# Fourier convolution with real and imaginary parts side by side, complex sums on VectorE and the inverse in row tiles

## The chip, the core and the metric

The kernel runs on one core of one Trainium2 chip. The metric is the time of one execution on the device in microseconds (us); the median of three runs stands for a kernel. The core has five engines that run their own queues in order and meet by semaphores: TensorE (PE, with its weight loads shown as PEld), VectorE (DVE), ScalarE (ACT), GpSimd (POOL) and SyncE (SP, here an issuer of DMAs). On-chip data lie in SBUF, and products of PE in the eight banks of PSUM, in both cases on 128 partitions.

## The reference

A block with two halves on 2048 rows of 576 channels: an S4 convolution and a gated MLP, each ahead of a residual and under scales from `c`. Cut to what matters here:

```python
mod = (_silu(c) @ w_mod).reshape(c.shape[0], 6, 1, -1)
h = _layernorm(x) * (1 + ca) + sa
P = exp(logdA[:, :, None] * l); K = einsum("dn,dnl,dn->dl", Cc, P, dB).real
Kf = rfft(pad(K, L)); Uf = rfft(pad(h.T, L))
y = irfft(Uf * Kf)[:L].T + h * Dskip          # L = 2048, transforms of 2L
x = x + ga * y
h = _layernorm(x) * (1 + cb) + sb
z = _gelu(h @ w_in); z1, z2 = z[..., :Fh], _layernorm(z[..., Fh:])   # Fh = 2304
x = x + gb * ((z1 * (w_sp @ z2 + b_sp)) @ w_out)
```

The change is in `y`: the transform of `h`, its complex product with `Kf`, and the inverse.

## The kernel before

Two parts follow one another. `ssm` (line 235) does the first residual, class `Mlp` the second, in `phase_a` (line 1370: layer norm, the second half of `w_in`, gelu, its layer norm) and `phase_b` (line 2149: the large products). The convolution is done in fp32 on PE as transforms in two steps, in five groups of channels (four of 128, one of 64) and in units, each a generator that stops at its `yield`s:

- e, t, p, k ("kg"), 1 ("k1") make the kernel's spectrum from the poles: exponentials and sines on ScalarE, `pg` products on VectorE, small products on PE (lines 561 to 690). They share time with the units below.
- `u_load`, `u_unit` (lines 706 and 711): a block of 512 columns (frequencies times channels) of the half-transformed `h` comes from DRAM as `u1`; one product with `fwd`, 128x128, gives the real parts in partitions 0 to 63 and the imaginary in 64 to 127 of a `pk` bank. ScalarE copies it into `uu[:, 0]`, and two DMAs from GpSimd's queue write the two halves swapped into `uu[:, 1]`.
- `z_unit` (line 722): the kernel's spectrum for the same 512 columns, products of `cst` with `k1`, into a `pk` bank; VectorE multiplies it with `uu` and with the swapped `uu` into `zz`, 128x1024.
- `v_unit` (line 733): two products over 512 columns with all 128 partitions of input, `inva` with `zz[:, 0]` and `invb` with `zz[:, 1]`, add up in one bank: the signs and sums of the complex product lie in the matrices (`st3a`, `st3b` in `consts`, line 131). ScalarE copies the bank to `v`, and a DMA of GpSimd's queue stores it in DRAM (`v_d`).
- `y_vload`, `y_xload`, `y_unit` (lines 745 to 790): SP's queue loads `v_d` again by rows, PE makes pairs of 128x64 products (in the records 128*64), VectorE adds them to `x`, and the sum goes to DRAM as `x1`; in the last groups of channels it also stays in SBUF (`x1f`, `x1l`, `xz`), so that phase A can start.

There are 36 units each of u, z and v (eight for a group of 128 channels, four for the last) and 20 of y.

The order is written out: string `ORDER` names one step after another, `Steps` (line 849) runs the unit named to its next `yield`, and `Pin` (line 212) keeps each engine's instructions in that order. All of them have the helper's line in the profile, L222, so one reads by tiles. Step D0 ends the making of the spectrum and starts `Mlp`. Steps L0 to L17 (list `late`) put first pieces of phase A among the last u, z, v and y: loads of `w_in` (`start_load`), its column sums and power-of-two scales (`start_sum`, `win_scale`), and its split in two fp16 parts (`start_hi` on ScalarE, `start_lo` on VectorE). The rest of these pieces stands at the start of `phase_a`, after `turn(0)`, the transposes of the first row tile. Which buffer of a ring each unit takes is written out too, in `PLAN`, by `Rings` (line 194): `uu` has four buffers of 128x2x512, `zz` two, `pk` four PSUM banks of 128x512.

Of the kernel before, what the change touches and what calls it, by code (L numbers as in the profile page):

```python
# [9 lines left out]
F32 = mybir.dt.float32  # L10
# [22 lines left out]
    "et": "0123401230243102431042341203420143201",  # L33
    "ft": "012012012120120210121021012102021021",
    "k1": "0101010",
    "kab": "010101001101010101001000111010110101",
    "pg": "010101101010101010110010101011010101",
    "pk": "01230123230123010123230130213020132013201320132013201023102312031203120312031203120312031202031203120312031023"
        "10231023102310231032132103210310210230210321031201321320130132103210230120120132120123102310312012301021302130"
        "12023013021013021301203123123023102023021321021302031203132103102312031203102310231023012312012031021302310231"  # L40
        "0231203121023120312013213201230130101010101010101010101010101010101010101",
    "ps": "01011011010101010101001010101111110101010101101010101011001101010110101010010101010101010101010101010101010101"
        "0101",
    "st1o": "010101010101010101",
    "u1": "0123401342304234130140320420124412032142102432402102401031024130",
    "uu": "01231032030313020231013020122030120123120",
    "v": "0101101010101101011010101010101010",
    "xb": "01100100101",
    "zz": "01011110110111010101010101101011011010",
# [3 lines left out]
B0 O0 O0 O0 O0 B2 O0 O0 O0 O0 B7 O0 O0 O0 O0 x0 O0 O0 O0 O0 O0 B1 O0 O0 O0 O0 O0 O0 S0 O0 O0 S0 i2 P0 S0 O0 O0 P0 O0 O0 B3 M2 S0 O0 P0 B5 Q0 i1 S0 M2 P0 S0 P0 e1 e0 P0 P0  # L53
e1 B6 P0 e0 B4 i0 e1 e0 t0 e1 g0 t1 M2 e0 P0 t1 t1 w3 M1 M1 M1 P0 P0 t2 M2 P0 M0 M1 M3 R1 R0 t1 t0 P0 t0 M0 M0 p1 t2 P0 p1 t0 p1 t2 j1 t2 e5 w4 M0 e2 M3 M3 p0 M0 p0 M0 e2
k1 p0 k1 e2 e2 k0 P0 M3 e3 11 M0 e5 P0 M0 11 11 O0 k0 M4 S1 e3 e5 p2 p2 g1 S1 M4 P0 S1 p2 e3 e6 M0 M4 e5 k2 O0 e4 e6 M3 P0 P0 e3 k2 M4 S1 A0 A0 R3 e4 R2 A0 t3 P0 A0 A0 A0
S1 A1 t3 S1 t5 A1 t3 O0 A1 A1 t5 A0 A1 A1 r2 t3 A1 t4 R5 A2 t5 A2 A2 R4 A2 e7 p3 A2 A2 A3 P0 t5 p3 P0 A3 M4 t4 r3 P0 A3 A3 10 p3 A3 t4 O0 A3 e8 12 R7 A2 j2 10 P0 e6 O0 t4
10 12 e4 p5 e7 k3 e4 e6 t8 12 k3 R6 e7 e7 A4 A4 A3 p5 e8 p5 t8 A4 p4 A4 A4 e8 e8 A4 S2 t7 A5 t8 S2 P0 A5 P0 A5 A5 S2 S2 S2 A5 P0 P0 A5 A4 t7 t7 P0 A6 t8 A6 A6 p4 t6 p4 A6
O0 A6 A6 A5 a5 t6 t6 A7 A7 A7 k4 t7 R10 a4 A7 R11 A7 A7 P0 k4 P0 13 w5 t6 13 14 Q1 13 P0 e10 p7 A6 14 k5 p7 A7 14 p7 M5 k7 e9 x3 e10 k5 M5 R8 P0 e11 k7 A8 e11 R9 p6 A8 A8
S3 A8 t10 A8 A8 S3 t10 S3 e9 S3 A9 A9 A9 A9 A9 e11 S3 p6 e10 r6 e10 p6 e9 t11 e9 A9 e11 Q2 A10 A10 R13 R12 p8 t10 A8 A10 A10 P0 A10 A10 17 k6 A9 p8 17 t11 p8 17 t10 M5 k6
t9 M5 t11 A11 A11 p10 t11 A11 P0 A10 e12 A11 15 A11 r7 t9 O0 p10 R15 t9 15 p10 A11 15 k8 k8 O0 A12 A12 e14 e12 p11 A11 p11 A12 A12 A12 A12 t14 A13 t14 A13 e14 P0 A13 M5  # L60
# [24 lines left out]
def consts():  # L85
# [46 lines left out]
    for h, sg in ((0, 1.0), (1, -1.0)):  # L132
        rows = slice(64 * h, 64 * h + 64)
        st3a[rows, 0::2] = sg * tr
        st3a[rows, 1::2] = -sg * ti
        st3b[rows, 0::2] = ti
        st3b[rows, 1::2] = tr
# [97 lines left out]
def ssm(tc, I, x1_d, consts_s, dram, mod_d, mlp):  # L235
# [6 lines left out]
    with ExitStack() as ctx:  # L242
# [314 lines left out]
        et = {}  # L557
# [1678 lines left out]
```

## Time and profile before

| | us |
|---|---|
| median of 3 runs (lowest to highest) | 1744.23 (1741.78 to 1744.63) |
| profiled execution, its own time | 1742.69 |
| its span | 1740.5 |
| PE busy | 1649.0 (95%) |
| VectorE busy | 1231.1 (71%) |
| ScalarE busy | 834.6 (48%) |
| GpSimd busy | 249.4 (14%) |

The span is what the profiler sees of the profiled execution, 2.2 us less than its time. "Busy" counts instructions that compute; a share over the whole span hides that the kernel has stages with different limits, so the stages must be read apart. In rows of the timeline a name such as `pk_b<-zz_b,small` is the output and the inputs, `128*64` the tile of PE, `x4` the number of records: an fp32 product has two.

### The profile page before, as it was taken

How to read it: one execution, taken by the hardware profiler on the slowest of the kernel's cores; microseconds unless marked ns; L12 is line 12 of the kernel's file. 1: busy time of each engine (PE TensorE's matmuls, PEld its weight loads, DVE VectorE, ACT ScalarE, POOL GpSimd, SP SyncE). 2: the span in 40 equal slices, each digit the busy share in tenths (PEclk: the TensorE clock that was granted, in tenths of full speed). 3: DMA queues.
4: the chain of work that ended last, by engine and by line, in shares of the span. 5: the costliest groups of instructions: out<-in, count | busy, mean ns of one | idle time of the engine just before them, and what ended most of it. 6: DMA issues, size and time to landing. Idle time of an engine off the chain costs nothing.

```text
span 1740.5 us, 38338 instructions
## 1 busy us (share of the span) xinstructions
PE 1649.0 (95%) x16158; PEld 1235.7 (71%) x16158; DVE 1231.1 (71%) x2179; ACT 834.6 (48%) x1202; POOL 249.4 (14%) x412
## 2 busy tenths in 40 slices
PE   3778999997999999999999999999999999999999
PEld 1344556664555446877878888888888888888887
DVE  6976888857999997888897867786444387334442
ACT  6979898762777565455443434343221233112210
POOL 3251323332222110000000000000111100111100
PEclk9878999998999999999999999999999999999999
DMA  9475946698798788676757786764667563556531
GB/s 240 141 214 179 276 118 202 198 292 242 226 308 265 227 249 294 243 250 241 248 161 237 273 298 241 266 213 144 241 225 234 197 217 105 194 198 213 194 108 42
DMA packets 182940, 376.43 MB, mean 216 GB/s; under 512 B 39104, under 2 KB 102976, under 8 KB 182000
## 3 DMA queue, kind: packets, MB, share of 16 engines
q1 hardware_dynamic: 138304, 168.56, 31.7%
q0 software_dynamic: 37984, 178.55, 31.1%
q10 hardware_dynamic: 6480, 26.86, 3.8%
q8 instruction: 127, 2.08, 0.5%
q14 instruction: 45, 0.37, 0.1%
HBM read 263.18 MB, written 101.31 MB: 209 GB/s over the span
## 4 chain that ended last, share of the span: by engine, by line
PE 66%; DVE 15%; DMA 6%; issue 3%; ACT 2%; POOL 0%; SPq 0%; ACTq 0%; DVEq 0%; POOLq 0%
PE ps L222 56%; PE pk_a L222 3%; PE pk_d L222 2%; PE pk_b L222 2%; DVE bsz L222 2%; DMA zset<-set_d 2%; PE pk_c L222 2%; DVE n L222 1%; DVE zset L222 1%; DVE rq L222 1%; DVE wsp L222 1%; DVE wso L222 1%; DVE gt L222 1%; DMA v_d<-v_a 1%; DVE nt L222 1%
## 5 line engine op out<-in xcount | busy, mean ns | idle before, releaser
L222 PEld LDWEIGHTS <-zset 128*128 128x128 f16 x7182 | 702.7, 98 | 92.4 <-DVE zset L222 7.2
L222 PE MATMUL ps<-wsp,zset 128*128 128x256 f16 x6048 | 669.0, 273 | 6.3 <-DVE zset L222 5.5
L222 PE MATMUL pz<-wz,nt 128*128 128x512 f16 (+1 forms) x1120 | 223.7, 359 | 8.9 <-ACT nt L222 3.5
L222 ACT ACTIVATE z<-gt 128x1024 f16<-128x1024 f32 x56 | 59.0, 1054 | 283.9 <-DVE gt L222 283.9
L222 PEld LDWEIGHTS <-nt 128*128 128x128 f16 x1120 | 109.4, 99 | 117.0 <-issue 5.0
L1944 POOL DMA_DIRECT2D zset<-set_d x96 | 50.8, 530 | 869.3 <-PE ps L222 608.1
L222 DVE SCALAR_TENSOR_TENSOR gt<-ps,sc,bsp 128x512 f32<-128x512 f32 x36 | 27.0, 749 | 205.4 <-PE ps L222 203.7
L222 PE MATMUL ps<-wout,z 128*128 128x288 f16 x1344 | 170.0, 286 | 0.0
L222 PEld LDWEIGHTS <-z 128*128 128x128 f16 x1344 | 131.5, 98 | 33.0
L222 PE MATMUL ps<-n2o,zset 128*128 128x256 f16 x1134 | 128.2, 273 | 0.0
L222 DVE TENSOR_TENSOR raw<-raw 128x512 f32<-128x512 f32 (+2 forms) x228 | 119.2, 528 | 12.0 <-DMA raw<-z_d 7.6
L222 DVE SCALAR_TENSOR_TENSOR gt<-ps,sc,gt 128x512 f32<-128x512 f32 (+1 forms) x180 | 122.2, 696 | 7.6
L222 ACT ACTIVATE zset<-raw 128x1792 f16<-128x1792 f32 x48 | 81.2, 1691 | 59.6 <-PE ps L222 25.0
L222 DVE TENSOR_TENSOR zset<-raw,zset 128x1792 f16<-128x1792 f32 x48 | 97.0, 2020 | 14.9 <-ACT zset L222 12.6
L222 DVE TENSOR_TENSOR z<-ps,z 128x512 f32<-128x512 f32 (+1 forms) x126 | 72.0, 599 | 36.8 <-ACT z L222 26.7
L222 ACT ACTIVATE wsp<-raw,sc 128x1792 f16<-128x1792 f32 x25 | 44.6, 1785 | 42.7 <-DVE raw L222 35.0
L222 ACT ACTIVATE z<-z,sc 128x1024 f32<-128x1024 f32 x21 | 24.1, 1148 | 75.6 <-DVE z L222 71.9
L222 ACT ACTIVATE z<-z,nm,r 128x1152 f32<-128x1152 f32 x24 | 31.5, 1342 | 53.6 <-DVE nm L222 30.3
L222 ACT ACTIVATE z<-pz,sc 128x512 f32<-128x512 f32 (+1 forms) x96 | 51.6, 583 | 10.2 <-DMA z_d<-z 7.2
L222 PE MATMUL ps<-n2q,wf 128*128 128x512 f16 x252 | 55.7, 379 | 0.0
L222 PE MATMUL ps<-wout,z1b 128*128 128x288 f16 x384 | 52.4, 286 | 0.0
L222 DVE SCALAR_TENSOR_TENSOR wsp<-raw,sc,wsp 128x1792 f16<-128x1792 f32 x25 | 51.9, 2078 | 0.0
(700 smaller groups left out, 2591.6 us busy)
## 6 DMA issues: line engine op xcount, KB each, us to landing
zset<-set_d POOLq DMA_DIRECT2D x96, 896.0 KB, 5.0
raw<-z_d SPq DMA_DIRECT2D x48, 512.0 KB, 5.5
set_d<-zset ACTq DMA_DIRECT2D x24, 896.0 KB, 6.1
z_d<-z POOLq DMA_DIRECT2D x32, 576.0 KB, 9.3
zset<-wa_d POOLq DMA_DIRECT2D x18, 896.0 KB, 4.9
raw<-in_w_spT SPq DMA_DIRECT2D x25, 512.0 KB, 4.5
set_d<-zset SPq DMA_DIRECT2D x12, 896.0 KB, 5.8
wst<-in_w_in SPq DMA_DIRECT2D x8, 1024.0 KB, 11.8
```

The costliest lines, as they stand in the source:

```text
L222: return self.tc.keep_in_program_order(f(*a, **k))
L1944: self.nc.gpsimd.dma_start(o, self.set_d[f, j - 1] if j else self.wa_d[f])
```

## The change

Real and imaginary parts now lie side by side in the free dimension, and the two halves of the 512 columns on the two halves of the partitions. For u, PE makes four products of 64 output rows over 256 columns; the copy to `uu` (now 128x512, eight buffers) is all that follows, and no DMA swaps. For z there are likewise products of 64 rows, twice as many. VectorE multiplies real and imaginary part of the spectrum with both parts of `uu` into `zz` (128x1024 as before), and after a further `yield` subtracts and adds quarters of it in place, 128x256 each. For v only the summed half of `zz` is read: four products with 64 partitions of input over 256 columns, two for each half of the partitions, in two `pk` banks, and two copies of 256 columns by ScalarE. The signs go out of `st3a`. The strings `ORDER` and `PLAN` are new, and seven pieces of phase A's start (`start_lo(2)`, `start_load(4)`, `start_sum(3)`, `win_scale(8)`, `start_hi(3)`, `ln2_two(1)` and its roots) become steps L18 to L24 in the convolution's last part. Of the two strings the diff shows a line or two.

```diff
@@ -30,55 +30,55 @@
 ROUNDED = set(range(14)) | set(range(15, 36, 2))
...
-    "uu": "01231032030313020231013020122030120123120",
+    "uu": "0123456710325076134052135170526047326034725136",
-    "zz": "01011110110111010101010101101011011010",
+    "zz": "01010010101100101001010101010101001101",
...
 ORDER = """
-u30 k32 133 k32 135 135 X10 132 135 u34 U24 v27 132 U32 132 y5 v26 D0 L4 L5 u24 U33 v27 u30 z34 v26 u24 L2 L9 v27 z30 z34 X16 u35 z30 z24 u24 u25 L3 v30 L0 v34 u35 z24
+v28 132 132 135 v28 135 v31 W8 135 z26 y8 W10 z27 D0 X17 L2 L0 z26 v27 y8 z26 L3 v27 z34 v26 z34 L4 v28 z24 z34 z24 v26 L5 z30 y10 z24 v34 L9 v34 z30 y10 z35 X18 z30 v26
...
@@ -129,10 +129,10 @@
     th = -2 * np.pi * np.outer(b4, k2) / 64
     tr, ti = np.cos(th).T, np.sin(th).T
     st3a, st3b = np.zeros((128, 128)), np.zeros((128, 128))
-    for h, sg in ((0, 1.0), (1, -1.0)):
+    for h in range(2):
         rows = slice(64 * h, 64 * h + 64)
-        st3a[rows, 0::2] = sg * tr
-        st3a[rows, 1::2] = -sg * ti
+        st3a[rows, 0::2] = tr
+        st3a[rows, 1::2] = -ti
         st3b[rows, 0::2] = ti
         st3b[rows, 1::2] = tr
     eye = np.eye(8)
@@ -688,13 +688,8 @@
         def part(n, bufs=2):
             return ring(sb, [128, 512], F32, n, bufs)
 
-        spare = []
-
         def half():
-            if not spare:
-                uu = ring(sb, [128, 2, 512], F32, "uu", 4)
-                spare.extend((uu[:, 1], uu[:, 0]))
-            return spare.pop()
+            return ring(sb, [128, 512], F32, "uu", 8)
 
         def by(t, c):
             return t.rearrange("p (k d) -> p k d", d=CHW[c])
@@ -711,34 +706,48 @@
         def u_unit(k):
             u1 = st.pop(k)
             pm = ps1()
-            T.matmul(pm, fwd, u1, start=True, stop=True)
+            for r in range(2):
+                for q in range(2):
+                    T.matmul(pm[64 * q:64 * q + 64, 256 * r:256 * r + 256], fwd[:, 64 * r:64 * r + 64], u1[:, 256 * q:256 * q + 256],
+                             start=True, stop=True, skip_group_check=True)
             yield
-            uu = st[k] = ring(sb, [128, 2, 512], F32, "uu", 4)
-            A.activation(uu[:, 0], pm, AF.Copy)
-            yield
-            G.dma_start(uu[:64, 1], uu[64:, 0])
-            G.dma_start(uu[64:, 1], uu[:64, 0])
+            uu = st[k] = ring(sb, [128, 512], F32, "uu", 8)
+            A.activation(uu, pm, AF.Copy)
 
         def z_unit(n):
             c, i = place(n)
             w = CHW[c]
             pm = ps1()
-            for j, k in enumerate(range(32)[kr(c, i)]):
-                T.matmul(pm[:, w * j:w * j + w], cst[k // 8][:, k % 8], k1t[c][:, k, :w], start=True, stop=True)
+            ks = range(32)[kr(c, i)]
+            m = len(ks) // 2
+            for j in range(m):
+                for r in range(2):
+                    for q in range(2):
+                        k = ks[m * q + j]
+                        T.matmul(pm[64 * q:64 * q + 64, 256 * r + w * j:256 * r + w * j + w], cst[k // 8][:, k % 8, 64 * r:64 * r + 64], k1t[c][:, k, :w],
+                                 start=True, stop=True, skip_group_check=True)
             yield
             uu = st.pop(n)
             zz = st[n] = ring(sb, [128, 2, 512], F32, "zz", 2)
-            V.tensor_tensor(zz, pm[:, None, :].to_broadcast([128, 2, 512]), uu, op=ALU.mult)
+            kk, u = (t.rearrange("p (r f) -> p r f", r=2) for t in (pm, uu))
+            p = zz.rearrange("p i (j f) -> p i j f", j=2)
+            V.tensor_tensor(p, kk[:, :, None, :].to_broadcast([128, 2, 2, 256]), u[:, None, :, :].to_broadcast([128, 2, 2, 256]), op=ALU.mult)
+            yield
+            V.tensor_tensor(p[:, 0, 0], p[:, 0, 0], p[:, 1, 1], op=ALU.subtract)
+            V.tensor_tensor(p[:, 0, 1], p[:, 0, 1], p[:, 1, 0], op=ALU.add)
 
         def v_unit(n):
             c, i = place(n)
             zz = st.pop(n)
-            pm = ps1()
-            T.matmul(pm, inva, zz[:, 0], start=True, stop=False)
-            T.matmul(pm, invb, zz[:, 1], start=False, stop=True)
+            pm = [ps1(), ps1()]
+            for r, m in enumerate((inva, invb)):
+                for q in range(2):
+                    rows = slice(64 * q, 64 * q + 64)
+                    T.matmul(pm[q][:, :256], m[rows], zz[rows, 0, 256 * r:256 * r + 256], start=not r, stop=r == 1, skip_group_check=True)
             yield
             v = half() if c == NC - 1 and i > 1 else part("v")
-            A.activation(v, pm, AF.Copy)
+            for q in range(2):
+                A.activation(v[:, 256 * q:256 * q + 256], pm[q][:, :256], AF.Copy)
             yield
             G.dma_start(v_d[c][:, kr(c, i)], by(v, c))
 
@@ -833,8 +842,11 @@
         late = [lambda: mlp.start_load(2), mlp.start_x1, lambda: mlp.start_sum(0), lambda: mlp.win_scale(5, False), lambda: mlp.start_sum(1),
                 lambda: mlp.win_scale(6, False), lambda: mlp.start_hi(0), lambda: mlp.start_hi(1), lambda: mlp.start_lo(0),
                 lambda: mlp.start_sums(ps2(), ps2()), lambda: mlp.start_lo(1), lambda: mlp.start_sum(2), mlp.start_rows,
-                lambda: mlp.start_load(3), lambda: mlp.win_scale(7), lambda: mlp.start_hi(2), lambda: first(0), lambda: mlp.ln2_rows(0)]
-
+                lambda: mlp.start_load(3), lambda: mlp.win_scale(7), lambda: mlp.start_hi(2), lambda: first(0), lambda: mlp.ln2_rows(0),
+                lambda: mlp.start_lo(2), lambda: mlp.start_load(4), lambda: mlp.start_sum(3), lambda: mlp.win_scale(8), lambda: mlp.start_hi(3),
+                lambda: pair.append(mlp.ln2_two(1)), lambda: pair[0]()]
+
+        pair = []
         once = {"B": begin, "w": lambda k: mod_load(k, S), "x": lambda k: ln_load(k, S), "i": lambda k: mod_load(k, G), "j": lambda k: ln_load(k, G), "r": lambda k: r1_load(k, S), "g": lambda k: r1_load(k, G),
                 "a": lambda k: r1_load(k, A), "Q": lambda k: poles_load(k, G), "C": middle, "c": cst_load, "f": st4_load, "b": lambda k: mlp.start_load(k, wpre),
                 "U": u_load, "W": y_vload, "X": y_xload, "D": end, "L": lambda k: late[k]()}
@@ -1433,19 +1445,12 @@
 
         self.turn(0)
         self.turn_hi(0)
-        self.start_lo(2)
-        self.start_load(4)
         self.x1_load(4)
         self.turn_lo(0)
-        roots12 = self.ln2_two(1)
         do(0, LD)
         self.z2_mm(0, 0)
         do(0, A0)
-        self.start_sum(3)
-        self.win_scale(8)
         self.z2_gelu(0, 0)
-        self.start_hi(3)
-        roots12()
         self.ln2_rows(1)
         do(0, PE)
         self.z2_mm(0, 1)
```

What the new strings do is seen in the order of the instructions. The first place is VectorE amid the convolution. `zz` are the products of z, `et`, `ft` and `pg` the making of the spectrum, `uu` and `pk` the two inputs of a product. Before:

```order
L222 TENSOR_TENSOR zz_b_2143<-pk_a_256,uu_a_2090 128x1024
L222 SCALAR_TENSOR_TENSOR et_e_115<-ft_a_380,et_e_115 128x16x32
L222 TENSOR_TENSOR et_e_115<-ft_a_380,et_e_115 128x16x32
L222 TENSOR_SCALAR ft_b_381<-ps_a_321 128x1024
L222 SCALAR_TENSOR_TENSOR ft_a_380<-ft_a_380,ps_b_322 128x1024
L222 TENSOR_TENSOR zz_a_2142<-pk_d_259,uu_d_2093 128x1024
L222 TENSOR_TENSOR zz_b_2143<-pk_b_257,uu_b_2091 128x1024
L222 TENSOR_TENSOR pg_b_474<-et_a_111,ft_c_382 128x1024 x2
```

In the new kernel, at about the same place:

```order
L222 TENSOR_TENSOR zz_b_2180<-pk_d_296,uu_b_2117 128x1024
L222 TENSOR_TENSOR pg_a_401<-et_c_113,ft_b_354 128x1024
L222 TENSOR_TENSOR zz_b_2180<-zz_b_2180 128x256 x2
L222 TENSOR_TENSOR pg_a_401<-et_c_113,ft_b_354 128x1024
L222 SCALAR_TENSOR_TENSOR ft_a_353<-ft_a_353,ps_a_275 128x1024
L222 SCALAR_TENSOR_TENSOR et_c_113<-ft_b_354,et_c_113 128x16x32
L222 TENSOR_TENSOR et_c_113<-ft_b_354,et_c_113 128x16x32
L222 TENSOR_TENSOR zz_a_2179<-pk_d_296,uu_d_2119 128x1024
L222 TENSOR_TENSOR pg_b_402<-et_b_112,ft_c_355 128x1024 x2
```

Behind each product now stands a pair of rows 128x256, the subtract and the add, with another unit's product between them and the product that they complete, or several.

The second place is VectorE at the turn from the convolution into phase A. The MEMSET of `wso` is phase A's first instruction, `wz` with `wst` the split of `w_in` (the number tells which piece), `nt` the transposed row tile, `bsx` statistics, `x1l` and `uu` here sums of y, `rq2` and `rx` the roots of two row tiles. Before:

```order
L222 TENSOR_TENSOR x1l_4466<-pk_b_257,x1l_4466 128x256
L222 TENSOR_TENSOR uu_c_2092<-pk_a_256,uu_c_2092 128x512
L222 TENSOR_TENSOR x1l_4466<-pk_d_259,x1l_4466 128x256
L222 MEMSET wso_4837 64x4x64
L222 SCALAR_TENSOR_TENSOR wz_4464<-wst_4535,sc_4458,wz_4464 128x4x512
L222 TENSOR_SCALAR wz_4464<-wst_4535,sc_4458 128x512
L222 SCALAR_TENSOR_TENSOR wz_4464<-wst_4535,sc_4458,wz_4464 64x512
L222 TENSOR_TENSOR nt_4845<-pt_4839,nt_4845 128x512
L222 TENSOR_TENSOR nt_4845<-pt_4839,nt_4845 64x128
L222 BN_STATS bsx_4862<-xz_4471 128x6 x2
L222 BN_AGGR mvx_4860<-bsx_4862 128x2
L222 BN_STATS bsx_4866<-xz_4471 128x6 x2
```

In the new kernel:

```order
L222 TENSOR_TENSOR rq2_5202<-rq2_5202,vh2_5201 128x2
L222 TENSOR_SCALAR rq2_5202<-rq2_5202 128x2
L222 TENSOR_TENSOR rx_5168<-rx_5168,rq2_5202 128x2
L222 TENSOR_TENSOR uu_b_2117<-pk_b_294,uu_b_2117 128x512
L222 TENSOR_TENSOR x1l_4754<-pk_a_293,x1l_4754 128x256
L222 MEMSET wso_5263 64x4x64
L222 TENSOR_TENSOR nt_5271<-pt_5265,nt_5271 128x512
L222 TENSOR_TENSOR nt_5271<-pt_5265,nt_5271 64x128
L222 SCALAR_TENSOR_TENSOR n2_5302<-xz_4759,mvx_5167,mrow_4750 128x576
L222 SCALAR_TENSOR_TENSOR n2_5302<-n2_5302,rx_5168,mrow_4750 128x576
L222 COPY n2_5302<-n2_5302 128x64
L222 SCALAR_TENSOR_TENSOR wz_4752<-wst_4904,sc_4746,wz_4752 128x4x512
```

The `wz` rows of `start_lo(2)` and the statistics `bsx` stood behind the MEMSET, ahead of and behind `nt`. Now the statistics and their roots stand ahead of it, as do the `wz` rows (further up than the rows shown), `n2` of the second row tile follows `nt` directly, and the next `wz` behind it is another piece.

More of the change, by code (lines that the diff above doesn't have):

```diff
@@ L82 @@
+v24 z32 L13 z35 L7 v24 L11 z25 z35 v35 v27 v35 L12 v30 v34 v30 z32 v24 L20 X11 z25 z32 z33 y8 z25 u33 W11 u33 X12 W5 L14 X16 X5 X19 L6 y10 v25 L21 v25 y11 v32 X13 X9 v30
+z33 y11 y5 v25 z33 v35 L8 L15 L1 v32 v33 v33 v32 W9 v33 L18 W12 y9 W13 W16 y5 W17 y12 L10 y12 X14 y16 y5 W14 y16 L16 y13 y17 y14 W15 y13 y14 L17 X15 L22 L23 W18 y15 y18
+y17 y11 y13 y14 y18 y9 L24 y15 y12 W19 y19 y16 y18 L19 y15 y19 y19 y9 y17
 """
```

77 lines of the change are left out of this document (37 added, 40 removed).

## The prediction

> **What bounds the kernel now.** I read the table by stages first. I cut the span at marks that a reader finds in the trace: the first product `zz` on VectorE (177.03 us), the MEMSET of `ones` with which step D0 opens the hand-off (356.19), the first transpose `pt<-ident` of phase A (412.18), and the first `ps` product of phase B (672.15). The columns are the stage and its length, then busy time and instructions of each engine, granted clock, DMA share and GB/s.
>
> ```profile
> core 0: us, PE busy (x) PEld busy (x) DVE busy (x) ACT busy (x) POOL busy (x), PEclk, DMA share, GB/s
> 0.00:177.03 177.03, 119.27 (x2016) 63.04 (x2017) 134.32 (x287) 146.52 (x275) 61.49 (x103) 0.85 0.67 194
> 177.03:356.19 179.16, 174.51 (x3206) 108.98 (x3207) 147.60 (x157) 151.12 (x232) 54.17 (x96) 1.00 0.70 201
> 356.19:412.18 55.99, 46.26 (x407) 31.01 (x395) 32.35 (x82) 24.45 (x32) 18.44 (x29) 0.94 1.05 299
> 412.18:672.15 259.97, 248.81 (x1320) 129.53 (x1319) 237.26 (x697) 173.15 (x264) 54.95 (x72) 0.99 0.80 249
> 672.15:1740.50 1068.35, 1060.14 (x9230) 903.09 (x9230) 679.52 (x959) 339.32 (x401) 60.36 (x114) 1.00 0.62 210
> ```
>
> The units u, z and v lie in the second and third row. In the second, PE works 174.51 of 179.16 us, at full clock: it is the bound, with 4.65 us idle, while VectorE has 31.56 us free. In the third no engine is the bound; the DMA share is 1.05, the highest of the five. Phase B is PE at 99% and isn't touched. The chain of waits by line, for the second and the third stage, says the same:
>
> ```profile
> by line: PE pk_a L222 19.7%; PE pk_d L222 19.1%; PE pk_b L222 17.1%; PE pk_c L222 15.9%; DMA cst<-in_c_st 6.1%; PE ps_b L222 4.6%; DMA v_d<-v_a 4.0%; PE ps_a L222 3.3%; DMA uu_c<-uu_c 3.1%; issue 2.6%; POOL uu_a L222 1.1%; DVE zz_b L222 0.7
> by line: issue 22.7%; DMA uu_b<-uu_b 13.7%; DMA uu_a<-v_d 11.1%; SPq L222 10.2%; DMA v_d<-v_a 9.5%; DMA uu_a<-uu_a 6.6%; POOL v_d L222 3.8%; PE pk_a L222 3.8%; PE pk_d L222 3.5%; PE pk_c L222 3.1%; POOL uu_b L222 2.6%; PE pk_b L222 2.5%; DV
> ```
>
> The stage is three quarters PE; the swap of halves (`uu<-uu`) is 3% of it. In the hand-off those swaps are 13.7 + 6.6 = 20.3%.
>
> **TensorE.** The next rows give the prices. The first is a piece of the chain of waits, one v unit (start, length). The others are from the timeline of PE (start, shown length, tile shape, records): a z, two u; then a v, the first and last pair of a y unit of 16 records, and what follows it.
>
> ```profile
> 183.26 1.72 PE pk_a L222 x4
> 377.10 1.11 PE L222 MATMUL pk_d<-k_b,cst 128*128 128x128 f32 x8
> 378.05 1.02 PE L222 MATMUL pk_b<-u_b,small 128*128 128x512 f32 x2
> 378.91 0.59 PE L222 MATMUL pk_c<-u_a,small 128*128 128x512 f32 x1
> ...
> 305.04 1.98 PE L222 MATMUL pk_a<-zz_b,small 128*128 128x512 f32 x4
> 306.96 0.32 PE L222 MATMUL pk_d<-u_e,st 128*64 128x128 f32 x1
> 306.96 0.32 PE L222 MATMUL pk_d<-u_b,st 128*64 128x128 f32 x1
> ...
> 307.78 0.27 PE L222 MATMUL pk_d<-u_b,st 128*64 128x128 f32 x1
> 307.98 0.39 PE L222 MATMUL pk_b<-sel,lb 112*128 112x512 bf16 x1
> ```
>
> From start to start, u costs 378.91 - 378.05 = 0.86 us and z 378.05 - 377.10 = 0.95. A v costs 1.72: two products over 512 columns, four records. The y unit shows what half-width tiles do: both records of a pair start at 306.96, and eight pairs pass by 307.78 + 0.11. So two 128x64 tiles side by side cost what one full tile costs for the same columns.
>
> The u and z of the new kernel are such pairs (four products of 256 columns; eight of 128): by the pairs above 2 x 0.43 and 4 x 0.21 us, so 0.86 each, no change. The new v is four products with 64 rows of input each, over 256 columns, in two row tiles. If these run side by side, that is two pairs of 0.43: 0.86, half of 1.72. No trace of before shows row tiles of this size over so many columns; the price lies between 0.86 and 1.72. I take 0.86, since the pairs of y are nearest, and keep 1.72 for a rival.
>
> Counted in the order of the instructions, from the first product to step D0, before and after have 27 v each, 30 and 35 u, and 9 and 7 y. PE loses 27 x 0.86 = 23.2 us and 2 x 0.86 for y, and gains 5 x 0.86 = 4.3 for u. A change of tile shape costs something as well: the v ends near 305.04 + 1.72 = 306.76 and the y starts 0.20 later; the y ends near 307.89 and the next shape starts 0.1 later. The order has 109 such changes in the stage before and 143 after; 34 x 0.15 = 5 us. PE is left with 174.5 - 23.2 - 1.7 + 4.3 + 5 = 159 us.
>
> The Trainium skill, page "TensorEngine Tiling (Array Packing)", section "Key Properties", says that changing the tiling mode, not merely the tile, drains TensorE. By that rule the mixed shapes speak against this change. The gaps of 0.20 and 0.1 us agree. With no cost for switches PE would have 154 us instead of 159, and rival three below would be 5 us lower; the forecast itself would not move, since PE isn't the bound in it.
>
> **VectorE.** These pairs of rows from its timeline give the price of a product and of a sum of 256 columns, from start to start; the last row is an add of y over 512 columns, 0.68 shown and some 0.6 with the same overlap.
>
> ```profile
> 240.09 1.22 DVE L222 TENSOR_TENSOR zz_b<-pk_d,uu_c 128x1024 f32<-128x1024 f32 x1
> 241.22 0.68 DVE L222 TENSOR_SCALAR ft_c<-ft_c 128x1024 int32<-128x1024 int32 x1
> ...
> 410.14 0.42 DVE L222 TENSOR_TENSOR x1l<-pk_b,x1l 128x256 f32<-128x256 f32 x1
> 410.48 0.68 DVE L222 TENSOR_TENSOR uu_c<-pk_a,uu_c 128x512 f32<-128x512 f32 x1
> ```
>
> The product still writes 128x1024, in runs of 256: 1.13 as before. What is new is the subtract and the add, 128x256 each. I take 0.34 us for one that follows straight on and 0.42, its shown length, for one that waits for the write ahead of it: 0.76 a unit, with 0.68 and 0.84 as ends. The stage before has 29 products, after it has 28, and two adds of y fewer: 147.6 - 1.13 - 1.2 + 28 x 0.76 = 166.5 us.
>
> **ScalarE and GpSimd.** A v leaves as two copies of 256 instead of one of 512:
>
> ```profile
> 227.72 0.60 ACT L222 ACTIVATE v_a<-pk_c 128x512 f32<-128x512 f32 x1
> 228.20 0.40 ACT L222 ACTIVATE kab_a<-pk_d 128x256 f32<-128x256 f32 x1
> 228.46 1.05 ACT L222 ACTIVATE et_e<-ps_b 128x1024 f32<-128x1024 f32 x1
> ```
>
> That is 2 x 0.26 for 0.48, 0.04 more; over 27 v, with five more u copies, ScalarE has some 154 us. GpSimd's queue loses the swaps of u, behind which the stores of v stood. With 54 busy of 179 us it bounds nothing, so this is worth only the waits that end with it.
>
> **The stage.** VectorE (166.5) takes PE's place (159) as the bound, ScalarE (154) close behind. How much idle will it keep? PE as the bound of this stage keeps 4.65 us; VectorE in phase A is busy 237.26 of 259.97, 91.3%, which here gives 182.4, or 15.9 idle. So 171 to 182; I take the middle, 10.3 idle: 176.8, or **-2.4 us**. The stage is nearly a draw: 23 us leave one engine and 21 go onto another.
>
> **The hand-off and the start of phase A** I take together, from D0 to `n` of phase A's second row tile, because the change moves work from the one into the other. The first row is this stretch in the table by stages, the next four are the swaps, the last store and its reload in the chain of waits, the rest is the work on VectorE's timeline that now goes ahead of the turn.
>
> ```profile
> 356.19:423.64 67.45, 56.88 (x450) 35.49 (x439) 42.69 (x117) 31.17 (x40) 22.92 (x35) 0.92 1.01 291
> 359.28 3.72 DMA uu_a<-uu_a
> 364.43 7.66 DMA uu_b<-uu_b
> 393.55 5.32 DMA v_d<-v_a
> 405.33 6.19 DMA uu_a<-v_d
> ...
> 413.11 2.35 DVE L222 SCALAR_TENSOR_TENSOR wz<-wst,sc,wz 128x2048 f16<-128x2048 f32 x1
> 416.56 1.00 DVE L222 TENSOR_TENSOR nt<-pt,nt 128x512 f16<-128x512 f32 x2
> 417.59 0.82 DVE L222 BATCH_NORM_STATS2 bsx<-xz 128x6 f32<-128x288 f32 x2
> 419.61 0.16 DVE L222 COPY sc<-pz 128x1 f32<-128x1 f32 x1
> 421.20 0.16 DVE L222 TENSOR_SCALAR vh<-mvx 128x2 f32<-128x2 f32 x1
> 423.64 0.81 DVE L222 SCALAR_TENSOR_TENSOR n<-xz,mvx,mrow 128x576 f32<-128x576 f32 x1
> ```
>
> Before, VectorE works from 413.11 to 416.56 on `start_lo(2)` (3.45 us), to 419.61 on statistics (2.0), to 421.20 on `win_scale(8)` (1.6) and to 423.64 on the root (2.4): 9.5 us after the turn, with PE waiting for the end of it. The change puts them ahead of the turn, where the last v goes through DRAM (5.32 and 6.19 us). Moved inside the stretch they don't change its sum of 42.69; added are eight subtract-add pairs (6.1), one more product (1.1) and two more adds of y (1.2): 51.1. Idle now is 67.45 - 42.69 = 24.8; of that 3.72 + 7.66 = 11.4 is the chain's wait for swaps, which are gone. 51.1 + 13.4 = 64.5, **-2.9 us**. If idle falls to phase A's share, it is 51.1 / 0.913 = 56.0, or -11.5; if all of it stays, +8.4.
>
> Moved too are ScalarE's part of `start_hi(3)`, PE's of `start_sum(3)`, and on SP's queue the loads: that of `start_load(3)`, 128x5x512 numbers or 1.3 MB, now stands ahead of the last reloads of v, 4.4 us at the 299 GB/s of this stretch. Against it stand fourteen swaps of 131 KB gone from here, 1.8 MB. I take nothing, from -2 to +4.
>
> **The sum.** Up to 177.03 the same units run in another order; five u copies of 0.48 us move out of it and other work comes in: 0, at most 3 either way. 1742.7 - 2.4 - 2.9 = 1737.4 on the profiled execution's own time (the span of 1740.5 and 2.2 around it), which is 1.5 under the median of the runs; I give 1738, between the two scales. A difference under 0.2% (3.5 us) can't be told from none here.
>
> **Rivals.** *Two, much faster:* the stretch of the turn falls to 56.0 and the stage to VectorE's 4.65 idle (-8.0): 1742.7 - 11.5 - 8.0 = 1723. For it: the swap waits are the longest of the hand-off's chain, and new orders were laid for both. Against: last store and reload remain, and 12 us of the 67 with them.
>
> *Three, it doesn't do what it says:* the row tiles of v do not run side by side. PE stays at 159 + 23.2 = 182, with its 4.65 idle 187: +7.7 - 2.9, 1747. Against: the column pairs of y do.
>
> *Four, slower:* VectorE keeps its idle. It is an in-order queue; now z has a product, a gap and two sums, v can't start before the second sum, the two banks of each v come out of a ring of four, and behind a product that waits for its bank stands every `pg` and `ft` step, on which PE's kernel generation waits. At today's 31.6 idle the stage is 198.1, +18.9: 1758.7. It decides from the idle: at 15.5 the whole kernel is even, at 19.0 it is 3.5 slower, at 12.0 3.5 faster. For it: three engines are loaded to 87-94% at once, where before only one was. Against: PE was kept at 97% by the same kind of order.
>
> **Chances.** Forecast, with 5 to 12 idle in the stage, 1732 to 1739: 0.40. Rival two, 1721 to 1732: 0.17. Idle of 12 to 19, so no difference: 0.16, 1739 to 1746. Rival three: 0.08, half of it within 0.2%. Rival four from 19 up: 0.19, of which a third lies under 1750. Faster by over 0.2%: 0.40 + 0.17 = 0.57; within: 0.16 + 0.04 = 0.20; slower: 0.04 + 0.19 = 0.23. The range from 1722 to 1750 leaves out a little of rival two and most of rival four.
>
> **What would show it.** In the profile of the changed kernel, a table with the same marks: VectorE 163 to 169 busy between the first `zz` and the MEMSET of `ones`, PE near 159, the stage 171 to 182; v records in pairs that start together, 0.86 a unit; sums of 128x256 with 0.34 to 0.42 each and little idle ahead of them; no `uu<-uu`; and `n` of the second row tile some 64 us after the MEMSET. I am wrong if v costs over 1.2 us, if VectorE's idle in the stage is over 15, or if the last reload of v lands later after D0 than the 55 us of now.

## The result and the profile after

The changed kernel takes 1719.24 us (median of four runs, 1717.41 to 1723.32) against 1744.43; the ratio is 0.9863, with a 95% interval from 0.985 to 0.9877. It is 25 us faster, where 6 had been forecast, and lies below the range. The profiled execution took 1718.49 us, its span 1716.7.

The same marks give these five stages in the changed kernel (columns as before):

```profile
0.00:166.90 166.90, 114.68 (x2050) 60.91 (x2053) 134.50 (x286) 143.94 (x272) 58.51 (x96) 0.86 0.69 202
166.90:333.20 166.30, 161.40 (x3726) 116.03 (x3724) 161.34 (x210) 154.63 (x266) 24.30 (x41) 0.99 0.60 175
333.20:389.67 56.47, 40.70 (x529) 31.60 (x527) 45.92 (x120) 27.18 (x42) 13.65 (x20) 0.86 0.98 290
389.67:648.70 259.03, 248.68 (x1319) 129.71 (x1317) 231.24 (x679) 169.19 (x261) 54.40 (x71) 0.99 0.81 245
648.70:1716.70 1068.00, 1059.95 (x9230) 903.20 (x9230) 679.52 (x959) 339.59 (x401) 60.62 (x114) 1.00 0.62 210
```

Stage by stage the span changes by -10.1, -12.9, +0.5, -0.9 and -0.4 us. In this execution all of the gain lies ahead of step D0: in the stage, and in the early part, in which hardly any unit was changed. The hand-off and phase A give nothing; a second execution, the last run below, has 4 us less there and 4 us more in the stage.

The chain of waits in the stage, by line, was three quarters PE. Now PE and VectorE take turns in it:

```profile
by line: PE pk_b L222 10.7%; PE pk_d L222 10.6%; PE pk_a L222 10.1%; PE pk_c L222 9.1%; DVE zz_a L222 8.4%; DVE pg_b L222 7.8%; issue 6.9%; DVE zz_b L222 6.9%; DVE pg_a L222 6.6%; DVE ft_a L222 3.2%; DVE ft_c L222 2.4%; DVE ft_b L222 2.4%; 
```

Cut finer, the middle of the stage shows why. This is one row of the table by stages, 80 us of it:

```profile
210.00:290.00 80.00, 79.41 (x1743) 55.73 (x1743) 79.93 (x105) 79.74 (x134) 9.33 (x16) 1.00 0.48 141
```

PE is busy 79.41 us of 80, VectorE 79.93 and ScalarE 79.74. Three engines that feed one another through two to eight buffers are full at the same time.

The prices were as forecast, or lower. On PE's timeline a v of the new kernel: both records of a pair start at 240.50, and four pairs take to 241.56, where the next shape starts.

```profile
240.50 0.48 PE L222 MATMUL pk_d<-zz_a,small 64*128 64x256 f32 x1
240.50 0.48 PE L222 MATMUL pk_a<-zz_a,small 64*128 64x256 f32 x1
...
241.25 0.38 PE L222 MATMUL pk_d<-zz_a,small 64*128 64x256 f32 x1
241.26 0.38 PE L222 MATMUL pk_a<-zz_a,small 64*128 64x256 f32 x1
241.56 0.24 PE L222 MATMUL pk_b<-dsk,small 128*32 128x4 f32 x8
```

That is 1.06 us with the change of shape in it, for 1.72 of old. On VectorE's timeline the sums of two units stand far behind their products:

```profile
239.71 0.75 DVE L222 TENSOR_TENSOR zz_a<-zz_a 128x256 f32<-128x256 f32 x2
240.38 0.75 DVE L222 TENSOR_TENSOR zz_b<-zz_b 128x256 f32<-128x256 f32 x2
241.06 1.22 DVE L222 TENSOR_TENSOR pg_a<-et_b,ft_b 128x1024 f32<-128x1024 f32 x1
```

A pair takes 0.68 us from start to start, not 0.76. Now the place where the 9.5 us moved out of phase A should have paid: the row tile `n` of VectorE, then, in a second fence, PE's timeline.

```profile
394.47 0.82 DVE L222 SCALAR_TENSOR_TENSOR n<-xz,mvx,mrow 128x576 f32<-128x576 f32 x1
```

```profile
389.67 1.33 PE L222 MATMUL pt<-ident,n 128*128 128x128 f32 x5
391.68 10.73 PE L222 MATMUL pz<-wz,nt 128*128 128x512 f16 x42 [0.69 <-ACT nt L222]
402.25 0.71 PE L222 MATMUL pt<-ident,n 128*128 128x128 f32 x5
```

`n` starts 61.3 us after D0, earlier than the 64 forecast and the 67.45 of before, and is done by 396.4. But its first reader, the second `pt` on PE, stands behind 42 products of the first row tile, and starts at 402.25, 69.0 us after D0. In the kernel before the same `pt`, behind as many products, started 69.3 us after D0, and had waited for `n` for no more than 0.40 us:

```profile
425.46 0.74 PE L222 MATMUL pt<-ident,n 128*128 128x128 f32 x5 [0.40 <-DVE n L222]
```

So there was next to nothing to be gained at `n`: what VectorE saves there waits for PE.

### The profile page after: what moved, and what is told of

Its sections match the earlier page's. It is cut to its first block, busy times and chain, and to the rows that moved or that the text cites. A ratio compares the mean times of both kernels' runs of the same rounds, so it can differ in the third digit from the quotient of the medians.

```text
span 1716.7 us, 39681 instructions
## 1 busy us (share of the span) xinstructions
PE 1625.4 (95%) x16838; PEld 1241.5 (72%) x16838; DVE 1252.5 (73%) x2251; ACT 834.5 (49%) x1239; POOL 211.5 (12%) x340
## 4 chain that ended last, share of the span: by engine, by line
PE 67%; DVE 19%; DMA 5%; ACT 4%; issue 4%; POOL 1%; SPq 0%; ACTq 0%; DVEq 0%; POOLq 0%
PE ps L222 58%; PE pz L222 3%; PE pk_c L222 1%; PE pk_b L222 1%; PE pk_d L222 1%; DVE bsz L222 1%; PE pk_a L222 1%; DVE zset L222 1%; DVE zz_a L222 1%; DMA zset<-set_d 1%; DVE n L222 1%; DVE pg_b L222 1%; DVE gt L222 1%; DVE zz_b L222 1%; DMA wsst<-in_w_spT 1%
## 5 line engine op out<-in xcount | busy, mean ns | idle before, releaser
L222 ACT ACTIVATE z<-pz,sc 128x512 f32<-128x512 f32 (+1 forms) x96 | 51.7, 583 | 19.7 <-PE pz L222 10.3
```

What stands on the lines that cost most here:

```text
L222: return self.tc.keep_in_program_order(f(*a, **k))
```

## The experiments

After the result there were three theories. *Whole order:* the new ORDER, not the new units, makes the gain. *Units:* less work on PE and no swaps make it, whatever the order. *VectorE alone:* the stage has one bound, VectorE, as forecast. Stages are read by the marks used so far; the measure for how far two executions of one kernel differ in them comes at the end of this section. Each ratio is to the kernel before as timed along with the run (medians from 1743.60 to 1745.99 us), so small differences are read from ratios.

**The new units on the old order.** ORDER, and the `late` list and phase A's start, are those of before (the helper's line is then L218), but for 26 of 1341 steps put off by one to five places and the strings of `pk` and `uu` in PLAN, dealt out to fit; the sums follow their product in one step:

```diff
-            yield
             V.tensor_tensor(p[:, 0, 0], p[:, 0, 0], p[:, 1, 1], op=ALU.subtract)
```

> The new u, z and v on the old order: ORDER and PLAN of before, with 26 of its 1341 steps put off by one to five places, because each v now holds two pk banks, the sums straight behind their product, and phase A's start as before. Theory 'order': most of the gain hangs on the new ORDER. The first u copy comes at 170 to 171 us as before, the first product some 174, and the convolution up to D0 takes 345 to 352 us (before 356, changed kernel 333); whole kernel 1733 to 1741. Rival 'units': the smaller PE work and the missing swaps bring all by themselves, whatever the order: D0 at 333 to 338, kernel 1719 to 1724.

Measured: 1752.88 us, ratio 1.0039 (1.0021 to 1.0057) to the kernel before. It is slower than before. Its row for the stage, and PE's longest waits there:

```profile
174.73:365.29 190.56, 170.51 (x3688) 117.73 (x3688) 168.54 (x216) 154.63 (x259) 24.83 (x42) 0.97 0.50 152
```

```profile
PE pk_c L218 <- DVE zz_b L218: 3.6, 3, 2.0
PE pk_a L218 <- issue: 3.0, 1, 3.0
PE pk_c L218 <- ACT et_e L218: 1.5, 1, 1.5
```

The stage is 190.56 us long, with VectorE idle for 22.0, PE for 20.1 and ScalarE for 35.9, and no one wait makes up a quarter of an engine's idle: a few us here, one there, in all three directions. The rival 'units' is out. The theory 'order' had the sign but expected 1733 to 1741: the units by themselves are worth less than it thought, namely a loss.

**Were the sums in the wrong place?** The same kernel with the `yield` back, and a third step of each z put into ORDER half way between its product and its v.

```diff
+            yield
             V.tensor_tensor(p[:, 0, 0], p[:, 0, 0], p[:, 1, 1], op=ALU.subtract)
```

> The new units on the old order again, now with the sums put off to half way between product and v (13.6 steps behind the product and 14.2 ahead of v, in the changed kernel 14.4 and 15.9). Theory 'whole order': 2 to 6 us better than with the sums at once, 1745 to 1751. Rival 'place of the sums': it takes back most of the loss, 1722 to 1735.

Measured: 1756.44 us, ratio 1.0076 (1.005 to 1.0103); its stage:

```profile
177.94:374.36 196.42, 174.23 (x3770) 121.85 (x3767) 166.24 (x215) 155.39 (x261) 25.73 (x44) 0.95 0.49 149
```

No better, where 'whole order' had expected 2 to 6 us of gain and the rival most of the loss back. And the other way round, in the changed kernel with the sums straight behind the product (the same edit as the diff above, and nothing else):

> The changed kernel with one thing undone: the subtract and the add stand straight behind their product instead of a dozen steps later; order and buffers otherwise as changed. Theory 'whole order': the wait for the product's write is 0.12 us a unit (1.26 from product to sum in the run of the new units on the old order, for 1.13 to any other instruction), so 3 to 7 us slower, 1722 to 1727. Rival 'place of the sums' (the old order is slow because the sums at once make every queue wait): 12 to 25 us slower, 1731 to 1745.

Measured: 1726.51 us, ratio 0.99 (0.9872 to 0.9929).

```profile
169.37:341.93 172.56, 162.87 (x3726) 116.42 (x3724) 164.86 (x210) 155.05 (x266) 24.21 (x41) 0.98 0.57 166
```

VectorE has 3.5 us more to do, as 28 x 0.12 says, and the stage is 2 to 6 longer than in the two executions of the changed kernel; the time is in the range of 'whole order'. (Five of the 28 pairs stand straight behind their own product in the changed kernel too.) The place of the sums is a small part of the matter.

**Was it the banks?** The runs on the old order had their `pk` banks dealt out by another rule. That rule alone in the changed kernel (only the string of `pk` in PLAN differs, of which the start is shown):

```diff
-    "pk": "012310231023102323102310230213102...
+    "pk": "012310230123012323012301231203012...
```

> The changed kernel with one thing altered: the PSUM banks of the ring pk are dealt out by the rule used for the runs on the old order (the free bank that was last read longest ago), which changes 247 of 400. Theory 'whole order' (the order of the steps is what counts): within 3 us of the changed kernel, 1717 to 1723. Rival 'banks' (the runs on the old order are slow because their banks were dealt out by this rule): 10 us slower or more.

Measured: 1725.76 us, ratio 0.9906 (0.9876 to 0.9936); the stage:

```profile
165.41:340.16 174.75, 162.85 (x3728) 115.90 (x3726) 162.37 (x210) 155.72 (x267) 24.46 (x41) 0.98 0.56 164
```

Neither theory's number: the rule costs some 6 us. That is a fifth of what lies between the changed kernel and its units on the old order, 1.0039 - 0.9863 of 1744 or 31 us.

**The early order alone.** The kernel before, with its first 480 steps in the new kernel's order (PLAN dealt out to fit, no unit changed; of ORDER the beginning is shown).

```diff
 ORDER = """
-B0 O0 O0 O0 O0 B2 O0 O0 O0 O0 B7 O0 O0 O0 O0 x0 O0 O0 O0 O0 O0 B1 O0 O0 O0 O0 O0 O0 S0 O0 O0 S0 i2 P0 S0 O0 O0 P0 O0 O0 B3 M2 S0 O0 P0 B5 Q0 i1 S0 M2 P0 S0 P0 e1 e0 P0 P0
+B0 B2 O0 g0 O0 O0 O0 O0 O0 O0 O0 B7 B3 x0 O0 B1 O0 O0 O0 O0 O0 O0 O0 O0 O0 B5 B4 O0 O0 O0 O0 S0 i2 P0 O0 O0 O0 O0 B6 O0 O0 O0 O0 S0 P0 Q0 S0 e1 S0 S0 e0 P0 e1 P0 e0 e0 P0
...
```

> The kernel before with one thing changed: its first 480 steps (all that stands ahead of the first u) come in the new kernel's order, the rest as it was. Theory 'order': the first u copy comes at 163 to 166 us instead of 170.75 and the end moves with it: 1736 to 1740. Rival 'units': the early part of the new kernel is shorter because fewer swaps share the queues and the DMA engines with it, so the order alone gives nothing: first u copy at 170 to 171, kernel 1742 to 1746.

Measured: 1739.76 us, ratio 0.9976 (0.9957 to 0.9996). The first u copy on ScalarE's timeline:

```profile
164.07 0.60 ACT L218 ACTIVATE uu_a<-pk_d 128x512 f32<-128x512 f32 x1
```

It is 6.7 us ahead of the 170.75 of before and equal to the 164.14 of the changed kernel. One execution is a weak witness here, as the last run of this section shows. But in all the profiles together this copy comes at 162.65 to 172.00 in the eleven runs with the new early order, 166.18 in the middle, and at 168.38 to 171.59 in the five with the old one, 170.93 in the middle. That and the median give the early order some 4 to 5 us.

**What the old units lost, in the old order.** First the swaps: the two DMAs are left out and z's product reads the unswapped half twice, so the cross terms are left out.

```diff
-            yield
-            G.dma_start(uu[:64, 1], uu[64:, 0])
-            G.dma_start(uu[64:, 1], uu[:64, 0])
...
-            V.tensor_tensor(zz, pm[:, None, :].to_broadcast([128, 2, 512]), uu, op=ALU.mult)
+            V.tensor_tensor(zz, pm[:, None, :].to_broadcast([128, 2, 512]), uu[:, 0:1].to_broadcast([128, 2, 512]), op=ALU.mult)
```

> The kernel before without the 72 DMAs that swap the halves of u; z's product reads the unswapped half twice, so the imaginary cross terms are left out. Theory 'order': the swaps stood in the way only where nothing else hid them, at the first product and in the hand-off: first product 2 to 4 us earlier, stage 176 to 179 since PE bounds it, hand-off 2 to 5 us shorter, kernel 1733 to 1740. Rival 'swaps': they are the main cause: 1720 to 1728. Rival 'hidden': no difference, 1742 to 1746.

Measured: 1733.77 us, ratio 0.9927 (0.9899 to 0.9954). The stage and the hand-off:

```profile
177.55:350.12 172.57, 172.56 (x3206) 108.92 (x3208) 147.71 (x157) 150.37 (x232) 24.83 (x42) 1.00 0.56 167
350.12:401.70 51.58, 44.65 (x407) 31.05 (x395) 32.34 (x82) 24.26 (x32) 11.91 (x17) 0.93 0.95 282
```

The stage falls from 179.16 to 172.57 and PE has no idle left; the hand-off falls by 4.4. So the swaps cost some 11 us, more than half of it in the stage. That 3.1% of its chain stood at `DMA uu_c<-uu_c` was to be read there: 5.6 us. The time is in the range of 'order', its places are not: the first product did not come earlier, and the stage had been put at 176 to 179.

Then, on top of it, half of v (`invb`'s product left out):

```diff
-            T.matmul(pm, inva, zz[:, 0], start=True, stop=False)
-            T.matmul(pm, invb, zz[:, 1], start=False, stop=True)
+            T.matmul(pm, inva, zz[:, 0], start=True, stop=True)
```

> As the one without swaps, and each v has one product instead of two (invb is left out), which takes 31 us from PE in the whole kernel and adds nothing to VectorE: what relief of PE alone is worth in the old order. Theory 'order': the old order itself, laid for a PE-bound stage, keeps the three engines waiting for each other: the stage falls from 179 to 166-172, not to the 153 of PE's work; kernel 1724 to 1733. Rival 'PE alone': the stage falls by all of 23 us and the kernel to 1712-1718.

Measured: 1724.3 us, ratio 0.9871 (0.9843 to 0.9899).

```profile
177.22:341.53 164.31, 154.89 (x3152) 99.25 (x3154) 147.57 (x157) 149.42 (x232) 24.84 (x42) 1.00 0.58 176
```

PE's work falls by 17.7 us, the stage by 8.3: not by all of it, as 'PE alone' had it, and by a little more than 'order' expected (166 to 172). With PE relieved, the old order keeps PE, VectorE and ScalarE idle for 9 to 17 us each.

**How many bounds has the new stage?** Four runs add work to one engine of the changed kernel, or take some away. VectorE without subtract and add (the complex sums left out):

```diff
-            V.tensor_tensor(p[:, 0, 0], p[:, 0, 0], p[:, 1, 1], op=ALU.subtract)
-            V.tensor_tensor(p[:, 0, 1], p[:, 0, 1], p[:, 1, 0], op=ALU.add)
```

> The changed kernel without the subtract and the add of z (the complex sums are left out): 36 x 0.68 = 24 us less for VectorE, 19 of it in the stage. Theory 'three bounds': PE and ScalarE hold the stage where it is: 1 to 6 us faster, 1713 to 1718. Rival 'VectorE alone': 12 to 20 us faster, 1699 to 1707.

Measured: 1721.68 us, ratio 0.9855 (0.9813 to 0.9897).

```profile
170.09:331.79 161.70, 157.65 (x3676) 114.00 (x3676) 144.44 (x154) 153.88 (x264) 23.53 (x40) 1.00 0.61 177
```

VectorE is rid of 16.9 us, the stage of 4.6, and the median doesn't differ. That is in neither theory's range, but far from the 12 to 20 us of 'VectorE alone'. VectorE with a second pair of sums on dead quarters:

```diff
+            V.tensor_tensor(p[:, 1, 0], p[:, 1, 0], p[:, 1, 1], op=ALU.subtract)
+            V.tensor_tensor(p[:, 1, 1], p[:, 1, 1], p[:, 1, 0], op=ALU.add)
```

> The changed kernel with a second pair of sums behind each pair, on the quarters of zz that nobody reads again: 24 us more for VectorE, 19 of it in the stage; the result is the same. Both theories: 14 to 24 us slower, 1733 to 1743. If VectorE had room (the 97% only apparent): under 6 us.

Measured: 1749.18 us, ratio 1.0007 (0.9982 to 1.0032).

```profile
168.95:357.88 188.93, 167.44 (x3764) 118.56 (x3760) 184.80 (x266) 158.76 (x269) 25.60 (x41) 0.98 0.53 155
```

Work of 23.5 us makes the stage 22.6 longer, and the time exceeds what both theories expected (1733 to 1743). PE, with the first pair of products of each v issued twice:

```diff
-            for r, m in enumerate((inva, invb)):
+            for r, m in ((0, inva), (0, inva), (1, invb)):
```

> The changed kernel with the first pair of products of each v issued twice (the second overwrites the first; the result is the same): 36 x 0.43 = 15 us more for PE, 27 x 0.43 = 11.6 of it in the stage. Theory 'three bounds': 8 to 14 us slower, 1727 to 1734. Rival 'VectorE alone bounds the stage': 0 to 5 us, 1719 to 1725.

Measured: 1730.17 us, ratio 0.9927 (0.9906 to 0.9949).

```profile
171.12:349.70 178.58, 172.00 (x3830) 126.03 (x3828) 162.75 (x211) 157.10 (x266) 24.17 (x41) 0.98 0.55 160
```

PE has 10.6 us more, the stage is 12.3 longer. ScalarE, with v's copies made twice:

```diff
-            for q in range(2):
+            for q in (0, 1, 0, 1):
                 A.activation(v[:, 256 * q:256 * q + 256], pm[q][:, :256], AF.Copy)
```

> The changed kernel with ScalarE's two copies of each v made twice (same result): 36 x 0.52 = 19 us more for ScalarE, 14 of it in the stage, where it has 11.7 us idle. Theory 'three bounds': 9 to 16 us slower, 1728 to 1736. Rival 'VectorE alone': what goes beyond ScalarE's idle, 2 to 5 us, 1720 to 1725.

Measured: 1735.46 us, ratio 0.9945 (0.9922 to 0.9968).

```profile
168.72:352.20 183.48, 167.24 (x3728) 118.71 (x3726) 163.17 (x210) 168.65 (x319) 24.46 (x41) 0.97 0.54 156
```

ScalarE has 14.0 us more, the stage is 17.2 longer. Against the ratio of the changed kernel the three times grow by 25, 11 and 14 us. Whichever engine is given more, the stage grows by about as much; VectorE, given less, brings little. The last two times are in the range of 'three bounds', and 'VectorE alone' is out.

**A run that tested something else.** v's four products issued tile by tile:

```diff
-            for r, m in enumerate((inva, invb)):
-                for q in range(2):
+            for q in range(2):
+                for r, m in enumerate((inva, invb)):
```

> The changed kernel with v's four products issued tile by tile (both of the first row tile, then both of the second) instead of in turns, so that only the middle two can run side by side: 1.29 us a v for 0.86, 27 x 0.43 = 12 us more for PE in the stage. Theory 'three bounds' (PE, VectorE and ScalarE are all at 93 to 99% in the stage): 8 to 14 us slower, 1727 to 1734. Rival 'VectorE alone bounds the stage': 0 to 4 us, 1719 to 1724.

Measured: 1723.6 us, ratio 0.9853 (0.9812 to 0.9893). By its number it would speak for VectorE alone. But PE's timeline shows that the edit didn't slow v:

```profile
213.93 0.48 PE L222 MATMUL pk_c<-zz_a,small 64*128 64x256 f32 x1
213.94 0.48 PE L222 MATMUL pk_b<-zz_a,small 64*128 64x256 f32 x1
...
214.68 0.38 PE L222 MATMUL pk_c<-zz_a,small 64*128 64x256 f32 x1
214.69 0.38 PE L222 MATMUL pk_b<-zz_a,small 64*128 64x256 f32 x1
214.89 0.39 PE L222 MATMUL ps_b<-sel 48*128 48x512 bf16 x2
```

The two tiles start 0.01 us apart although their products were issued one tile after the other: 0.96 us for the whole v. So this run says nothing about PE as a bound; the run with the doubled product took its place.

**The late steps back.** L18 to L24 out of ORDER and of the list (and one bank, with the shifts behind it, out of the end of `pk`), and at the start of phase A again:

```diff
         self.turn_hi(0)
+        self.start_lo(2)
+        self.start_load(4)
         self.x1_load(4)
         self.turn_lo(0)
+        roots12 = self.ln2_two(1)
...
+        self.start_sum(3)
+        self.win_scale(8)
         self.z2_gelu(0, 0)
+        self.start_hi(3)
+        roots12()
```

> The changed kernel with steps L18 to L24 back at the start of phase A, as in the kernel before; all else as changed. Theory 'PE-bound phase A': PE has 249 us of work in its 259 and takes back what VectorE gains ahead of it: within 2 us of the changed kernel, 1717 to 1722. Rival (the prediction): the nine microseconds of VectorE's work after the turn are worth 3 to 6 us: 1722 to 1726.

Measured: 1724.56 us, ratio 0.9868 (0.9836 to 0.99). The time lies in the range of the rival, which was the prediction, the ratio 1 us from the changed kernel; so it must be read from the stages. From D0 to phase B, in the changed kernel and, in the next fence, with the steps back:

```profile
333.20:648.70 315.50, 289.38 (x1845) 161.31 (x1843) 277.16 (x798) 196.37 (x303) 68.05 (x90) 0.97 0.84 253
```

```profile
339.81:657.18 317.37, 290.32 (x1840) 161.81 (x1839) 277.14 (x798) 194.73 (x300) 67.28 (x90) 0.97 0.83 251
```

That is 1.9 us more, and 5.8 more than in the second execution below (311.61). In the other runs that keep the late steps in place this stretch takes up to 320.94 (the one with v issued tile by tile), so no gain of the late steps can be told from the spread. PE comes to the second `pt` 69.7 us after D0 without them, 69.0 and 68.6 with: 1 us at most.

**The changed kernel again,** with no edit.

> The changed kernel once more, nothing altered, as the measure for the runs that differ from it by 2 to 7 us: its early part up to the first u copy took 164.1 us in its profile, and 166 to 172 in the seven runs whose early part is word for word the same. Theory 'spread': first u copy at 165 to 171, kernel 1719 to 1725. Rival 'fixed': 164 again and 1717 to 1720, so that the other runs lose early for a reason of their own.

Measured: 1719.89 us, ratio 0.987 (0.9843 to 0.9896). Its stage and the stretch from D0 to phase B:

```profile
166.62:336.93 170.31, 163.46 (x3730) 117.36 (x3728) 161.73 (x211) 155.16 (x267) 24.95 (x41) 0.98 0.58 169
336.93:648.54 311.61, 287.72 (x1840) 160.40 (x1839) 277.09 (x798) 195.94 (x301) 67.34 (x90) 0.98 0.85 256
```

Single stages of one kernel differ by 4 us between two executions (170.31 and 166.30; 311.61 and 315.50), and the sum of the two by 0.1. So a single stage above is good to some 4 us, and the growths of 12 to 23 stand well clear of it. The first u copy came at 163.85 and the time at 1719.89, the numbers of the rival 'fixed'. But in the seven runs whose early part is the same word for word it had come between 165.95 and 172.00, and the edits of these stand behind it; so up to 8 us of their early part is not theirs, and what it hangs on wasn't found. They ran on two other chips than the repeat; the kernel before differs by less than 2 us between these three, but that a chip has a part in it is not excluded. This spread is why the runs that lie 2 to 7 us from the changed kernel are read by their stages and not by their times alone.

## Why the prediction was wrong

**The sign and the prices held.** v in row tiles costs about half, 36 pairs of sums cost 0.68 to 0.76 each, no swap is left; PE has 161.40 us of work in the stage where 159 was worked out. The 5 us set down for changes of tile shape fit that: without them 154 would have stood there, though a sum can't tell them from a dearer v. What the Trainium skill says on the page "TensorEngine Tiling (Array Packing)", section "Key Properties", that a change of mode drains TensorE, agrees with it as far as a sum can.

**The first step that failed** is "How much idle will it keep? ... I take the middle, 10.3 idle: 176.8, or -2.4 us". The stage took 166.30, and 170.31 in the second execution: VectorE's work came to 161.34 and 161.73 instead of 166.5, and its idle to 5.0 and 8.6. Of the 5 us of work too many, 28 x 0.08 = 2.2 are the price of a pair, 0.68 and not 0.76: sums that stand far behind their product don't wait for it, and put straight behind it they cost 3.5 more in the run above. The rest was not taken apart. The stage lies at or under the lower end of the range: the new order keeps VectorE nearly as full as the old one kept PE. The choice of the middle between two rows gave away 2 to 5 us, VectorE's work priced too high another 5. Rival two, with 171, was nearest in the stage. That its total, 1723, is near as well is luck: the early part's -10.1, which it had at nothing, stands in for the -11.5 that it expected at the turn and that did not reach the end.

**The second** is "the same units run in another order [...] 0, at most 3 either way". An order was treated as neutral where no unit changed. The early part became 10.1 us shorter. Up to the first u copy it is 6.6 in this profile, and 4 in the median of the run that has nothing else. The other 3.5 lie between that copy and the first product: 2.76 us instead of 6.28, which stayed 6.28 without swaps and 6.35 with the new units on the old order, so neither of these alone is what shortened it.

**The third** is the hand-off with the start of phase A, -2.9, of which nothing arrived (-0.5 from D0 to phase B; -4.4 in the second execution, of which the second `pt`, at 68.6 us, accounts for 0.7). The step that failed is "with PE waiting for the end of it": PE waited for `n` for 0.40 us, and it was busy for 248.81 of phase A's 259.97 us. The row that gives this share was quoted. `n` came earlier, as forecast, and `pt` behind it at 69.0 us after D0 for 69.3. That more than half of what the swaps cost fell in the stage, and not in the hand-off, was missed as well.

**What the forecast had no term for** is the whole order as a cause of its own. In steps of the measured ratios, times 1744: no swaps -13, half of v -10, then the sums and the rest of the new units, still on the old order, +29; then the new order with its banks -31. Rival four ("VectorE keeps its idle", 31.6 us, stage 198) is what the units alone did: 22 idle and 190.6, 30 and 196.4 in the two runs. It did not come true because the order was laid anew for them.

**What stays open.** That these units lose on the old order and gain on the new one is shown: the order as a whole, with the buffer plan that goes with it, decides. Of its traits, the early part (some 4 us), the place of the sums (2 to 6 us of the stage) and the banks (some 6) were tried and are a part. What makes the other 15 to 19 was not taken apart: ahead of D0, u runs further ahead (84 steps on average from its copy to its product, 72 before), and the shortest way from a product to its v is 13 steps instead of 2, but no run alters one of these alone. Of PLAN, only `pk` was dealt out otherwise. Nor did the old units get a new order in the stage, so how much of the 25 us they could have had is not known. In the stage it can't be all: there PE alone had 174.51 us of work with them, more than the 166.30 and 170.31 that the new stage takes.

## What to carry to other kernels

When a change takes work from the bound engine and gives nearly as much to another, its worth is decided by the order of the queues: the same units were 0.4% slower on the old order and 1.4% faster on one laid for them, so judge a new layout only with its own order. Price the idle of the new bound by what the old bound kept in the same kind of order, not by a middle between distant rows. And follow a gain to the next reader on the busiest engine before counting it: what VectorE finished by 396.4 us was not read until 402.25, behind 42 products of PE.

## What the runs showed of the hardware

Row tiles of PE ran side by side even where the kernel issues the products of one tile after those of the other: starts 0.01 us apart, 0.96 us for a v of four products. The order of issue is read from the kernel there; the trace shows the starts. The Trainium skill, page "TensorEngine Tiling (Array Packing)", section "Key Properties", says that different tiles can work in parallel. The trace agrees. On VectorE, an instruction that reads what the product just ahead of it writes started 1.25 us behind that product's start, one that reads something else 1.13 (240.09 to 241.22 in the kernel before), so the wait for the write is 0.12 us. The 1.25 is to be seen in the run of the new units on the old order:

```profile
234.00 1.22 DVE L218 TENSOR_TENSOR zz_b<-pk_c,uu_c 128x1024 f32<-128x1024 f32 x1
235.25 0.76 DVE L218 TENSOR_TENSOR zz_b<-zz_b 128x256 f32<-128x256 f32 x2
235.93 1.22 DVE L218 TENSOR_TENSOR zz_a<-pk_d,uu_d 128x1024 f32<-128x1024 f32 x1
```
